# One schedule of attention groups over all blocks, with more of the transposes moved from TensorE to the DMA

## The chip, the cores and the metric

The kernel runs on one NeuronCore of a Trainium2 chip. The metric is device time in microseconds (us), the median of several executions. The engines that matter are TensorE (PE, whose weight loads are listed as PEld), VectorE (DVE), ScalarE (ACT) and SyncE (SP), which here only issues DMAs. Each engine works through its own instructions in the order of the program.

## What is computed

The reference chains three stages on 2304 tokens of width 512.

```python
# 1. attention in chunks of 64 tokens, 4 batches x 8 heads x 576 tokens x 64
scores = scale * q_c @ k_c^T ; scores -= max ; attn = exp(scores)
attn = attn / (sum(attn) + 1e-9) ; out = attn @ v_c
# 2. MLP1, d_ff = 2048
h = x @ w_in ; g = max(h, 0) + alpha * min(h, 0) ; x = g @ w_out
# 3. MLP2, d_ff = 1536
x = ((x @ w_a) * (x @ w_b)) @ w_out2
```

## The kernel before

**Precision by splitting.** Every matrix product of the MLPs is made of three matmuls, high times high, high times low and low times high (`three`, L366). A helper splits a float tile into a high part on ScalarE (`to_hi`, L79) and a low part on VectorE (`to_lo`, L82). The weights come as 64-bit numbers and are unpacked before they are split: ScalarE widens them (L124), VectorE does three steps (L128, L133, L136). A loaded weight tile of 512 KB is called a unit; there are 32 units for MLP1 and three staging buffers (tag `stg`) for units on their way.

**Blocks and steps.** The tokens are cut into five blocks of 512, 256, 512, 512 and 512 tokens. MLP1 runs block by block; a block has 16 steps `j`. In a step TensorE multiplies `x` with one column tile of `w_in` (`s1`, result in a PSUM bank `psh`), ScalarE and VectorE form the PReLU and its two parts (L384, L385, L386, then `gh` and `gl`), and TensorE multiplies these with a row tile of `w_out` two steps later (`s2`, into the four banks `acc`). During block 0 the step is `prelu_unpacking`: it also unpacks two units of weights, in an order written out by hand across ScalarE and VectorE, and loads two further ones. MLP2 follows for all blocks; the change does not touch it.

**Attention in groups.** 128 tokens are a group; there are 18 groups, numbered `u`, four in a block of 512 and two in block 1. For a group the kernel needs q and k transposed (`kT`, `qT`), scores (`att_S`, 32 small matmuls, L291), maximum and subtraction on VectorE (`att_M`), exponential on ScalarE (`att_X`, L312), normalization on VectorE (`att_N`, L317 to L321), the transpose of the result (`eT`, `att_PT`), and the product with v (`att_O`, 32 small matmuls, L342). The result is split into the `x` of its block.

**Two ways to transpose.** On TensorE, four transposes of 128x128 go to a PSUM bank and ScalarE copies that out (`att_T`, L278 and L280, for q and k; `att_PT`, L330 and L332, for e). Through the DMA, ScalarE first parts the 32-bit numbers into 16-bit halves (`halves`, L242, 128x1024), SP writes these to DRAM (L244), and a DMA transpose reads them back (`turned`, L249). Before the change groups 0 to 5 have q and k transposed on TensorE and groups 6 to 17 through the DMA (`apart`, then `turn_qk`); e is transposed on TensorE for groups 0 to 9 and through the DMA from `P_DMA = 10` on.

**Where the attention work stands.** The groups of block 0 come first, in an order written out by hand. The groups of block `b + 1` are worked on during the 16 steps of block `b`, at numbered slots, two in a step: an even slot `2j` is taken inside step `j`, in block 0 just behind the two PReLU reads of ScalarE, and an odd slot `2j + 1` at the end of the step, behind `s2`. `att_steps` gives the list of slots of one block; some actions return work that is done a little later in the step (`settle`). Block 0 takes the groups 4 and 5 (scores of both together in `both_S`, products of both in `both_O`), block 1 takes the groups 6 to 9 with a lag of one group between scores and product, and blocks 2 and 3 take four groups each with a lag of two.

**Buffers.** Four PSUM banks (`bank`) are shared by `psh`, the transposes and the pairs of banks of scores and products.

Of the kernel before, what the change touches and what calls it, by code (L numbers as in the profile page):

```python
# [8 lines left out]
F32 = mybir.dt.float32  # L9
# [9 lines left out]
def chunk_attention_prelu_mlp_bilinear_mlp(  # L19
# [18 lines left out]
    P = 128  # L38
# [29 lines left out]
    def bank(nm="ps"):  # L68
        return ps_p.tile([P, DM], F32, tag="ps", name=nm)
# [5 lines left out]
    def wtile(name, dt=F32R):  # L75
        return wp.tile([P, DM], dt, tag="w", name=name)
# [88 lines left out]
    def weave(*chains):  # L165


        live, later = [], [iter(c) for c in chains]
        while live or later:
            if later:  # L170
                live.append(later.pop(0))
            live = [c for c in live if next(c, None) is not None]
# [26 lines left out]
    def half(i):  # L199
        return slice(i * CH, (i + 1) * CH)  # L200
# [29 lines left out]
    def load_v(u):  # L230
        load("v", u)
# [2 lines left out]

    P_DMA = 10

    def halves(src, dst, nm):

        d = dst.bitcast(U16).rearrange("p (t f) -> p t f", t=2)
        nc.scalar.activation(out=d, in_=src.bitcast(U16).rearrange("p (f t) -> p t f", t=2), func=AF.Copy)  # L242
        rows = dr.tile([P, 2, DM], U16, name=f"rows{nm}")
        nc.sync.dma_start(out=rows, in_=d)  # L244
        return rows

    def turned(rows, nm):
        t = wtile(nm, F32)
        nc.sync.dma_start_transpose(  # L249
            out=t.bitcast(U16).rearrange("p (g r) -> p g r", g=KD), in_=rows.rearrange("p t f -> (p t) f")  # L250
        )
        return t
# [5 lines left out]
    def turn_qk(u):  # L258
        for nm, rows in zip("kq", att.pop(("rows", u))):
            t = turned(rows, f"{nm}T{u}")  # L260
            att[nm + "T", u] = lambda r, g, c, t=t: t[r, half(2 * g + c)]

    n_early = [0]

# [46 lines left out]
    def att_X(u):  # L311
        nc.scalar.activation(out=att["e", u], in_=att["e", u], func=AF.Exp, scale=SCALE)  # L312
# [9 lines left out]

    def att_PT(u):
        e_ = att.pop(("e", u))
        if u >= P_DMA:
            att["eT", u] = turned(halves(e_, wtile(f"ed{u}", F32), f"e{u}"), f"eT{u}")
            return
        ps = att_bank(u, "psP")
        for g in range(KD):
            nc.tensor.transpose(ps[:, g * P:(g + 1) * P], e_[:, g * P:(g + 1) * P], ident)  # L330
        t = wtile(f"eT{u}", F32)
        nc.scalar.activation(out=t, in_=ps, func=AF.Copy)  # L332
        att["eT", u] = t
# [18 lines left out]
    def each(fn, parts):  # L352
        for part in parts:
            fn(*part)
# [150 lines left out]
        while len(pend) > lag:  # L505
            pend.pop(0)()

    def att_steps(b, x):

        t0, n = blocks[b]
        us = range(t0 // P, (t0 + n) // P)

        def multiply(w, lag):
            pss = [bank("psSO") for _ in range(2)]
            now, before = us[w:w + 1], us[max(w - lag, 0):max(w - lag + 1, 0)]
            for u in now:
                att_S(u, [ps[:, :KD * CH] for ps in pss])
            o = []  # L520
            for u in before:
                o += att_O(u, *x, u * P - t0, [ps[:, KD * CH:] for ps in pss])
                if u + 2 < NU:
                    load_v(u + 2)
            each(to_hi, o)

            def then():
                for u in now:
                    att_M(u)
                each(to_lo, o)  # L530

            return then

        def soften(u):
            att_X(u)
            return lambda: weave(att_N(u))

        def both(product, us):
            pss = [bank("psSO") for _ in range(2)]
            return [product(u, [ps[:, i * KD * CH:(i + 1) * KD * CH] for ps in pss]) for i, u in enumerate(us)]  # L540

        def both_S():
            both(att_S, us)
            return lambda: att_M(us[0])

        def both_O(us):
            o = sum(both(lambda u, pss: att_O(u, *x, u * P - t0, pss), us), [])
            each(to_hi, o)
            for u in us:
                if u + 2 < NU:  # L550
                    load_v(u + 2)
            return lambda: each(to_lo, o)

        def nothing():
            pass

        def only(fn, *a):
            def step():
                if a[0] < NU:
                    fn(*a)  # L560
                return nothing

            return step

        if b == 1:
            u0, u1 = us
            return [
                (8, only(att_T, u0)),
                (10, only(att_T, u1)),
                (10, only(load_kq, u1 + 1, False)),  # L570
                (14, both_S),
                (16, lambda: lambda: att_M(u1)),
                (18, lambda: soften(u0)),
                (20, lambda: soften(u1)),
                (21, only(apart, u1 + 1, False)),
                (24, only(att_PT, u0)),
                (24, only(att_PT, u1)),
                (24, only(turn_qk, u1 + 1)),
                (25, only(load_kq, u1 + 2)),
                (27, lambda: both_O(us)),  # L580
                (28, only(apart, u1 + 2)),
                (29, only(load_kq, u1 + 3)),
                (30, only(turn_qk, u1 + 2)),
            ]
        u = us[0]
        if sizes[b - 1] < NB:
            S_, lag = {
                "m": (0, 7, 14, 21, 28), "s": (2, 9, 16, 23), "p": (6, 13, 20, 27),
                "l": ((4, 3), (11, 4), (18, 5), (29, 6)), "a": ((1, 2), (8, 3), (15, 4), (24, 5)), "t": ((4, 2), (11, 3), (25, 4), (29, 5)),
            }, 1  # L590
        else:
            S_, lag = {
                "m": (0, 6, 12, 18), "s": (2, 8, 14, 20), "p": (4, 10, 16, 22),
                "l": ((3, 3), (9, 4), (15, 5), (24, 6)), "a": ((1, 2), (7, 3), (15, 4), (23, 5)), "t": ((3, 2), (13, 3), (21, 4), (29, 5)),
            }, 2
        steps = [(slot, lambda w=w: multiply(w, lag)) for w, slot in enumerate(S_["m"])]
        steps += [(slot, lambda w=w: soften(us[w])) for w, slot in enumerate(S_["s"])]
        steps += [(slot, only(att_PT, us[w])) for w, slot in enumerate(S_["p"])]
        if lag == 2:
            steps += [(28, lambda: both_O(us[-2:]))]  # L600
        for i, fn in enumerate((load_kq, apart, turn_qk)):
            steps += [(slot, only(fn, u + n)) for slot, n in S_["lat"[i]]]
        return sorted(steps, key=lambda s: s[0])

    with tc.manual_schedule():
# [57 lines left out]
        to_hi(*wparts[3])  # L663
        nc.scalar.mul(nalpha_sb, alpha_sb, -1.0)

        for b, (t0, n) in enumerate(blocks):
            nxt = xtiles("x")
            steps = att_steps(b + 1, nxt) if b + 1 < NBLK else []

            def advance(slot, steps=steps):  # L670
                rest = []
                while steps and steps[0][0] <= slot:
                    rest.append(steps.pop(0)[1]())
                return rest

            def settle(rest):
                for then in rest:
                    then()

            for j in range(J1):  # L680
                if b == 0:
                    if j in (1, 3):
                        load_qk(n0 + j // 2)
                    if j in (4, 6):
                        load_v(n0 + j // 2 - 2)
                h = h0[0][:, :n] if not (b or j) else s1(j, x, n)
                if b == 0:
                    g = prelu_unpacking(j, h, lambda: w_dma(min(2 * j + 9, NU1)), lambda: advance(2 * j), settle)
                else:
                    rest = advance(2 * j)  # L690
                    g = prelu(j, h)
                    settle(rest)

                def second(b=b, j=j, g=g, n=n, nxt=nxt):
                    if j == 0:
                        acc[0] = new_acc()
                    s2(j, g, acc[0], n)
                    if j == J1 - 1:
                        end1(b, acc[0], n, nxt)

                pend.append(second)
                flush(2)
                settle(advance(2 * j + 1))
                if b == NBLK - 1 and j >= 2:
                    ready = NU1 + 3 * (j - 2) // 2
                    w_dma(ready + 3)
                    w_unpack(ready + 1)
                    w_split(ready)
            x = nxt
# [60 lines left out]
```

## Time and profile before

| | |
|---|---|
| median of 3 runs | 897.88 us (897.57 to 898.58) |
| the profiled execution | 897.61 us, span 895.8 us |
| TensorE | 884.1 us busy, 99% |
| VectorE, ScalarE | 402.7 us and 352.6 us, 45% and 39% |
| DMA | 79.48 MB, mean 89 GB/s |

The page divides the span into 40 slices of 22.4 us; attention and the unpacking of MLP1's weights lie in the first 16 or so, and behind them TensorE works alone. Block 0 of MLP1 runs from about 25 us to 118 us, block 1 to 173 us. A granted TensorE clock of 1.00 is the full 2.4 GHz.

### The profile page before, as it was taken

The numbers are of one execution on the slowest core, as the hardware profiler recorded it, in microseconds if no ns is written. First come the engines' busy times: TensorE is split into PE (matmuls) and PEld (weight loads), VectorE is DVE, ScalarE is ACT, GpSimd is POOL, SyncE is SP. The second block draws the span as 40 slices with busy tenths as digits, with TensorE's granted clock in tenths as the row PEclk, the third lists the DMA queues.
The fourth block names the chain that finished last, engine by engine and source line by source line (L and its number), as shares of the span: only waits on it lengthen the run. The fifth ranks groups of instructions, "written<-read, shape, count | busy, mean of one in ns | idle before, by whom it ended". The sixth has DMA issues, their size and how long they took to land.

```text
span 895.8 us, 12893 instructions
## 1 busy us (share of the span) xinstructions
PE 884.1 (99%) x5298; PEld 743.9 (83%) x5298; DVE 402.7 (45%) x762; ACT 352.6 (39%) x636; POOL 0.7 (0%) x6
## 2 busy tenths in 40 slices
PE   7999999999999999999999999999999999999998
PEld 6878889988888888888888888888888888888897
DVE  5999955454434443388756742111211122111221
ACT  5687765555436343466534422111211122111211
POOL 0000000000000000000000000000000000000000
PEclk9899999999999999999999999999999999999999
DMA  9686767455425320444414312000020002000100
GB/s 213 199 263 196 213 165 178 107 155 129 106 60 146 79 56 5 141 142 141 148 64 136 124 46 93 2 1 0 1 95 1 0 1 71 1 1 0 48 1 23
DMA packets 127498, 79.48 MB, mean 89 GB/s; under 512 B 94160, under 2 KB 116176, under 8 KB 127440
## 3 DMA queue, kind: packets, MB, share of 16 engines
q1 hardware_dynamic: 127152, 78.41, 31.0%
q8 instruction: 41, 0.67, 0.3%
q10 hardware_dynamic: 288, 0.26, 0.1%
q14 instruction: 17, 0.14, 0.1%
HBM read 53.49 MB, written 16.78 MB: 78 GB/s over the span
## 4 chain that ended last, share of the span: by engine, by line
PE 92%; DVE 6%; ACT 2%; issue 1%; ACTq 0%; POOLq 0%; DVEq 0%; POOL 0%
PE psh L366 52%; PE acc L366 37%; DVE wx L136 1%; PE psSO L291 1%; PE psSO L342 1%; DVE wz L128 1%; DVE wz L133 1%; DVE gl L82 0%; PE psT L278 0%; DVE sm L317 0%; PE warm L625 0%; PE psP L330 0%; DVE e L321 0%; DVE mx L304 0%; DVE e L306 0%
## 5 line engine op out<-in xcount | busy, mean ns | idle before, releaser
L442 DVE TENSOR_TENSOR b_sb<-psh,b_sb 128x512 f32<-128x512 f32 (+1 forms) x60 | 38.3, 638 | 273.2 <-PE psh L366 273.2
L386 DVE SCALAR_TENSOR_TENSOR pos<-neg,nalpha_sb,pos 128x512 f32<-128x512 f32 (+1 forms) x80 | 55.6, 695 | 107.3 <-ACT pos L385 107.0
L440 ACT ACTIVATE b_sb<-psh 128x512 f32<-128x512 f32 (+1 forms) x60 | 33.1, 552 | 168.2 <-PE psh L366 168.2
L79 ACT ACTIVATE ch<-b_sb 128x512 fp32r<-128x512 f32 (+1 forms) x60 | 35.3, 589 | 153.6 <-DVE b_sb L442 153.6
L82 DVE TENSOR_TENSOR gl<-pos,gh 128x512 fp32r<-128x512 f32 (+1 forms) x80 | 51.1, 638 | 43.5 <-ACT gh L79 43.5
L79 ACT ACTIVATE gh<-pos 128x512 fp32r<-128x512 f32 (+1 forms) x80 | 47.2, 590 | 59.0 <-DVE pos L386 59.0
L384 ACT ACTIVATE neg<-psh 128x512 f32<-128x512 f32 (+1 forms) x80 | 43.8, 548 | 40.4 <-PE psh L366 40.4
L82 DVE TENSOR_TENSOR cl<-b_sb,ch 128x512 fp32r<-128x512 f32 (+1 forms) x60 | 38.3, 639 | 39.3 <-ACT ch L79 39.3
L136 DVE SCALAR_TENSOR_TENSOR wx<-wx,wz 128x512 int32<-128x512 int32 x68 | 46.8, 689 | 4.7 <-ACT wx L124 0.8
L124 ACT ACTIVATE wx<-raw 128x512 f32<-128x512 f32 x68 | 42.7, 669 | 4.0 <-DMA raw<-in_moe_w_b_dram 3.8
L385 ACT ACTIVATE pos<-psh 128x512 f32<-128x512 f32 (+1 forms) x80 | 44.2, 553 | 0.0
L128 DVE TENSOR_SCALAR wz<-raw 128x512 uint16<-128x512 uint16 x68 | 29.8, 462 | 3.2 <-DMA raw<-in_moe_w_b_dram 3.2
L133 DVE TENSOR_SCALAR wz<-raw 128x512 uint16<-128x512 uint16 x68 | 31.0, 455 | 0.0
L242 ACT ACTIVATE kqd<-kq 128x1024 uint16<-128x1024 uint16 x24 | 23.9, 1047 | 0.3 <-DMA kq<-in_k_dram 0.3
L79 ACT ACTIVATE xh<-psSO 128x256 fp32r<-128x256 f32 x28 | 8.9, 384 | 25.0 <-PE psSO L342 25.0
L312 ACT ACTIVATE e<-e 128x512 f32<-128x512 f32 x18 | 11.3, 629 | 13.6 <-DVE e L306 13.4
L242 ACT ACTIVATE ed<-e 128x1024 uint16<-128x1024 uint16 x8 | 8.5, 1058 | 17.2 <-DVE e L321 13.6
L321 DVE TENSOR_TENSOR e<-e,rc 128x512 f32<-128x512 f32 x18 | 12.4, 691 | 0.6
L317 DVE TENSOR_REDUCE sm<-e 128x8 f32<-128x512 f32 x18 | 12.2, 680 | 1.0 <-ACT e L312 0.8
L82 DVE TENSOR_TENSOR xl<-psSO,xh 128x256 fp32r<-128x256 f32 x28 | 10.2, 415 | 1.5 <-ACT xh L79 1.5
L304 DVE TENSOR_REDUCE mx<-psSO 128x4 f32<-128x256 f32 x28 | 10.5, 418 | 0.7 <-ACT xh L79 0.7
L291 PEld LDWEIGHTS psSO<-kT,qT 64*64 64x64 f32 x448 | 7.7, 134 | 3.7 <-issue 2.8
(731 smaller groups left out, 2505.7 us busy)
## 6 DMA issues: line engine op xcount, KB each, us to landing
raw<-in_moe_w_out_dram SPq DMA_DIRECT2D x28, 512.0 KB, 3.5
raw<-in_moe_w_in_dram SPq DMA_DIRECT2D x16, 512.0 KB, 4.6
raw<-in_moe_w_b_dram SPq DMA_DIRECT2D x12, 512.0 KB, 4.7
raw<-in_moe_w_a_dram SPq DMA_DIRECT2D x12, 512.0 KB, 3.8
v<-in_v_dram SPq DMA_DIRECT2D x16, 256.0 KB, 4.2
out_dram<-os SPq DMA_DIRECT2D x8, 512.0 KB, 2.8
rowsk<-kqd SPq DMA_DIRECT2D x12, 256.0 KB, 2.1
rowsq<-kqd SPq DMA_DIRECT2D x12, 256.0 KB, 2.5
```

What stands on the lines that cost most here:

```text
L79: nc.scalar.activation(out=hi, in_=src, func=AF.Copy)
L82: nc.vector.tensor_tensor(out=lo, in0=src, in1=hi.bitcast(F32), op=ALU.subtract)
L124: return nc.scalar.activation(out=x.bitcast(F32), in_=hw.bitcast(F32), func=AF.Copy, scale=2.0 ** -112)
L128: yield nc.vector.tensor_scalar(out=z2[:, :, 0], in0=h2[:, :, 1], scalar1=13, scalar2=None, op0=ALU.logical_shift_right)
L133: yield nc.vector.tensor_scalar(out=z2[:, :, 1], in0=h2[:, :, 3], scalar1=1 << 15, scalar2=None, op0=ALU.bitwise_and)
L136: yield nc.vector.scalar_tensor_tensor(out=x, in0=x, scalar=3, in1=z, op0=ALU.logical_shift_left, op1=ALU.bitwise_or)
L366: nc.tensor.matmul(out=ps, lhsT=a, rhs=b, start=(i == 0 and first), stop=(i == n_i - 1 and a is wl))
L384: nc.scalar.activation(out=neg, in_=h, func=AF.Relu, scale=-1.0)
L385: yield nc.scalar.activation(out=pos, in_=h, func=AF.Relu)
L386: yield nc.vector.scalar_tensor_tensor(out=pos, in0=neg, scalar=nalpha_sb[:, j:j + 1], in1=pos, op0=ALU.mult, op1=ALU.add)
L440: nc.scalar.activation(out=b_sb, in_=pb, func=AF.Copy)
L442: nc.vector.tensor_tensor(out=b_sb, in0=pa, in1=b_sb, op=ALU.mult)
```

## The change

The two functions of a list of slots per block become one function, `att_schedule`, with one line of slots over all blocks (32 slots to a block, `PER`). In it:

- q and k of groups 4 and 5 are loaded with `load_kq` where `load_qk` was, and transposed through the DMA: `apart` at slots 6 and 9, `turn_qk` at slots 8 and 11. `att_T` is left to block 0.
- e goes through the DMA from group 6 on (`apart_e`, `turn_e` as steps of their own); `att_PT` is left to groups 0 to 5.
- The scores of groups 4 and 5 move from slot 14 to 16, `att_M` of 5 from 16 to 17. `apart` of 6 moves from slot 21 to 18, of 7 from 28 to 25, and that of group 8 into block 0 (slot 30). The first scores of block 1's work (group 6) move from slot 32 to 31.
- From group 6 on every scores step carries the product of the group two before, across the borders of blocks; the last scores of a block's work no longer stand at its beginning, and `both_O` at the end of blocks 2 and 3 is gone.
- In a joint step the low parts of the product come before `att_M`, where they came behind it.

```diff
-    P_DMA = 10
+    def apart_e(u):
+        att["rows_e", u] = halves(att.pop(("e", u)), wtile(f"ed{u}", F32), f"e{u}")
+
+    def turn_e(u):
+        att["eT", u] = turned(att.pop(("rows_e", u)), f"eT{u}")
...
     def att_PT(u):
         e_ = att.pop(("e", u))
-        if u >= P_DMA:
-            att["eT", u] = turned(halves(e_, wtile(f"ed{u}", F32), f"e{u}"), f"eT{u}")
-            return
...
+    PER = 2 * J1
+    def multiply(now, before):
+        pss = [bank("psSO") for _ in range(2)]
+        if now is not None:
+            att_S(now, [ps[:, :KD * CH] for ps in pss])
+        o = []
+        if before is not None:
+            o = outputs(before, [ps[:, KD * CH:] for ps in pss])
+        each(to_hi, o)
+
+        def then():
+            each(to_lo, o)
+            if now is not None:
+                att_M(now)
+        return then
...
+        u = sizes[0] // P
+        do(6, apart, u, False)
+        do(8, turn_qk, u)
+        do(9, apart, u + 1, False)
+        do(11, turn_qk, u + 1)
+        do(10, load_kq, u + 2, False)
+        at(16, both_S, u, u + 1)
+        at(17, lambda: lambda: att_M(u + 1))
+        do(18, apart, u + 2, False)
+        at(18, soften, u)
+        do(21, turn_qk, u + 2)
+        at(20, soften, u + 1)
+        do(20, load_kq, u + 3, False)
+        do(24, att_PT, u)
+        do(24, att_PT, u + 1)
+        do(25, apart, u + 3)
+        do(26, turn_qk, u + 3)
+        at(27, both_O, u, u + 1)
+        do(28, load_kq, u + 4)
+        do(30, apart, u + 4)
+        at(31, multiply, u + 2, None)
+        at(36, multiply, u + 3, None)
...
+        when = {u + 3: 31}
+        for b in range(1, NBLK - 1):
+            us = [w for w in range(NU) if group_block[w] == b + 1]
+            for w, s in zip(us, (11, 17, 23, 29) if sizes[b] < NB else (8, 15, 22, 29)):
+                when[w + 2] = b * PER + s
+        for w, s in list(when.items())[1:]:
+            at(s, multiply, w if w < NU else None, w - 2)
+            if w >= NU:
+                continue
+            at(s + 2, soften, w)
+            do(s + 4, apart_e, w)
+            if w > u + 4:
+                do(when[w - 1] + 1, turn_qk, w)
+            do(s + 8, turn_e, w)
+            if w > u + 5:
+                do(when[w - 2] + 3, apart, w)
+            if w > u + 6:
+                do(when[w - 3] + 4, load_kq, w)
...
                     if j in (1, 3):
-                        load_qk(n0 + j // 2)
+                        load_kq(n0 + j // 2, False)
```

## Rows read from the trace of the kernel before

**Rows 1.** The page, part 1: busy us (share of the span) and instructions.
```profile
PE 884.1 (99%) x5298; PEld 743.9 (83%) x5298; DVE 402.7 (45%) x762; ACT 352.6 (39%) x636; POOL 0.7 (0%) x6
```

**Rows 2.** Busy time by stretch: length, PE, PEld, DVE, ACT, POOL, clock, DMA share, GB/s.
```profile
45.00:70.00 25.00, 24.37 (x174) 19.87 (x173) 24.06 (x47) 19.69 (x36) 0.00 (x0) 1.00 0.90 265
70.00:95.00 25.00, 25.00 (x112) 20.72 (x111) 24.77 (x53) 17.24 (x32) 0.00 (x0) 1.00 0.53 172
...
135.00:173.00 38.00, 38.00 (x452) 37.40 (x452) 21.40 (x54) 22.62 (x53) 0.00 (x0) 1.00 0.71 160
```

**Rows 3.** Timeline of PE in block 0: start, us, work, wait before it.
```profile
47.76 0.60 PE L278 MATMUL psT<-ident,k 128*128 128x128 f32 x4
...
48.55 0.48 PE L366 MATMUL acc<-gh,wo2h 128*128 128x512 f32 x1
...
54.89 0.66 PE L278 MATMUL psT<-ident,k 128*128 128x128 f32 x4 [0.63 <-ACT pos L385]
...
55.79 0.48 PE L366 MATMUL acc<-gh,wo3h 128*128 128x512 f32 x1
...
96.29 0.63 PE L330 MATMUL psP<-ident,e 128*128 128x128 f32 x4 [0.40 <-DVE e L321]
```

**Rows 4.** Chain of waits, pieces in order of time: start, us, what.
```profile
93.77 0.60 DVE wx L136
94.38 0.61 DVE sm L317
...
95.45 0.70 DVE e L321
96.15 0.14 issue
96.29 0.63 PE psP L330 x4
```

**Rows 5.** Timeline of DVE and ACT in block 0.
```profile
49.96 0.74 DVE L386 SCALAR_TENSOR_TENSOR pos<-neg,nalpha_sb,pos 128x512 f32<-128x512 f32 x1
...
54.72 0.60 ACT L280 ACTIVATE kT<-psT 128x512 f32<-128x512 f32 x1
...
55.19 0.74 DVE L386 SCALAR_TENSOR_TENSOR pos<-neg,nalpha_sb,pos 128x512 f32<-128x512 f32 x1
...
55.68 1.26 ACT L124 ACTIVATE wx<-raw 128x512 f32<-128x512 f32 x2
...
59.84 0.59 ACT L385 ACTIVATE pos<-psh 128x512 f32<-128x512 f32 x1
...
60.79 0.73 DVE L386 SCALAR_TENSOR_TENSOR pos<-neg,nalpha_sb,pos 128x512 f32<-128x512 f32 x1
...
66.38 0.74 DVE L386 SCALAR_TENSOR_TENSOR pos<-neg,nalpha_sb,pos 128x512 f32<-128x512 f32 x1
```

**Rows 6.** Timeline of ACT: two halves, and two widenings at two places.
```profile
65.90 1.46 ACT L124 ACTIVATE wx<-raw 128x512 f32<-128x512 f32 x2
...
71.14 1.24 ACT L124 ACTIVATE wx<-raw 128x512 f32<-128x512 f32 x2
...
94.95 1.99 ACT L242 ACTIVATE kqd<-kq 128x1024 uint16<-128x1024 uint16 x2
```

**Rows 7.** Timeline near the end of block 0, DVE and PE.
```profile
117.49 0.69 DVE L82 TENSOR_TENSOR gl<-pos,gh 128x512 fp32r<-128x512 f32 x1 [0.70 <-ACT gh L79]
...
119.28 0.50 PE L366 MATMUL acc<-gh,wo14h 128*128 128x512 f32 x1
```

**Rows 8.** DMA issues: what, count, KB each, median us to landing.
```profile
rowsk<-kqd SPq DMA_DIRECT2D x12, 256.0 KB, 2.1
...
kT<-rowsk SPq DMA_TRANSPOSE x12, 4.0
qT<-rowsq SPq DMA_TRANSPOSE x12, 3.5
```

**Rows 9.** Chain of waits around block 1, pieces in order of time.
```profile
118.73 0.62 PE psSO L291 x32
...
142.79 0.44 PE psP L330 x4
...
145.28 0.47 PE psSO L342 x32
145.75 1.63 PE acc L366 x12
147.38 1.44 PE psh L366 x12
```

**Rows 10.** Timeline of DVE and PE at the start of block 2.
```profile
186.31 0.75 DVE L459 COPY xs<-acc 128x256 f32<-128x256 f32 x2
...
186.78 0.50 PE L366 MATMUL acc<-gh,wo0h 128*128 128x512 f32 x1
```

More of the change, by code (lines that the diff above doesn't have):

```diff
@@ L506, in flush @@
             pend.pop(0)()
[L508 to L602, printed above, removed]
@@ new lines, in chunk_attention_prelu_mlp_bilinear_mlp @@
+    PER = 2 * J1
+    group_block = [b for b, n in enumerate(sizes) for _ in range(n // P)]
+    xof = {}
+    def multiply(now, before):
[11 more added lines that the diff above has]
+        return then
@@ new lines, in outputs, with soften, both_S, both_O @@
+    def outputs(u, pss):
+        b = group_block[u]
+        o = att_O(u, *xof[b], u * P - blocks[b][0], pss)
+        if u + 2 < NU:
+            load_v(u + 2)
+        return o
+    def soften(u):
+        att_X(u)
+        return lambda: weave(att_N(u))
+    def both_S(*us):
+        pss = [bank("psSO") for _ in range(2)]
+        for i, u in enumerate(us):
+            att_S(u, [ps[:, i * KD * CH:(i + 1) * KD * CH] for ps in pss])
+        return lambda: att_M(us[0])
+    def both_O(*us):
+        pss = [bank("psSO") for _ in range(2)]
+        o = []
+        for i, u in enumerate(us):
+            o += outputs(u, [ps[:, i * KD * CH:(i + 1) * KD * CH] for ps in pss])
+        each(to_hi, o)
+        return lambda: each(to_lo, o)
@@ new lines, in att_schedule, with at, do @@
+    def att_schedule():
+        steps = []
+        def at(slot, fn, *a):
+            steps.append((slot, lambda: fn(*a)))
+        def do(slot, fn, *a):
+            steps.append((slot, lambda: fn(*a) and None or (lambda: None)))
+        u = sizes[0] // P
[20 more added lines that the diff above has]
+        at(36, multiply, u + 3, None)
+        do(37, turn_qk, u + 4)
+        at(33, soften, u + 2)
+        do(33, load_kq, u + 5)
+        at(38, soften, u + 3)
+        do(35, apart_e, u + 2)
+        do(40, apart_e, u + 3)
+        do(37, turn_e, u + 2)
+        do(39, apart, u + 5)
+        do(42, turn_e, u + 3)
+        do(40, load_kq, u + 6)
+        when = {u + 3: 31}
[16 more added lines that the diff above has]
+                do(when[w - 3] + 4, load_kq, w)
@@ L664, in chunk_attention_prelu_mlp_bilinear_mlp, with advance @@
         nc.scalar.mul(nalpha_sb, alpha_sb, -1.0)
+        steps = att_schedule()
         for b, (t0, n) in enumerate(blocks):
-            nxt = xtiles("x")
-            steps = att_steps(b + 1, nxt) if b + 1 < NBLK else []
-            def advance(slot, steps=steps):
+            nxt = xof[b + 1] = xtiles("x")
+            def advance(slot, t=b * PER):
                 rest = []
-                while steps and steps[0][0] <= slot:
+                while steps and steps[0][0] <= t + slot:
                     rest.append(steps.pop(0)[1]())
```

## The prediction

> **What bounds the kernel now.** I began with the page's busy shares: TensorE is busy for 99% of the span and the other engines for less than half [rows 1]. Read alone, this says that whatever is taken off TensorE is gained. That holds only where TensorE does not wait for someone else soon after, so the second view is the busy time by stretches [rows 2]. From 45 to 95 us, in block 0, VectorE is busy for 24.06 and 24.77 of each 25 us: there it is as full as TensorE. From 135 to 173 us, in block 1, TensorE has 38.00 of 38.00 us and VectorE only 21.40. So there are two regimes, and the change works in both.
>
> The third view is the chain of waits. In block 0 it runs through VectorE (unpacking, normalization) up to e of group 5, which ends at 96.15 us, and there TensorE takes it over with the transposes of e, for which it had waited [rows 3, 4]. So at 96 us, behind the whole stretch of unpacking, TensorE's place in time is set by VectorE. What TensorE saves earlier in block 0 turns into a longer wait at this point; what delays VectorE earlier moves the point back.
>
> In block 1 the chain is TensorE's own work, piece behind piece [rows 9].
>
> **The change, part by part.**
>
> *Transposes of q and k of groups 4 and 5 off TensorE.* They take 48.55 - 47.76 = 0.79 us for the one group and 0.63 + 0.90 us for the other, the 0.63 being a wait for a bank; with 0.1 us of slower start of the matmuls behind each the sum is 2.5 us [rows 3]. I count this as 0, because TensorE meets e of group 5 afterwards. The cover is VectorE's fullness; if that is gone, it is worth -2.5.
>
> *What ScalarE gets instead.* A pair of evictions of transposes goes and a pair of halves comes, for each group. In the hand-written order of block 0 both engines form one loop: VectorE's `pos` of one step to that of the next. A step without evictions takes 55.19 - 49.96 = 5.23 us; the two with evictions take 5.60 and 5.59 us [rows 5]. So the evictions cost the loop 0.73 us in all, which is now saved. A pair of halves takes 1.99 us [rows 6].
> - Group 4, slot 6: the halves stand where the evictions stood, before the two widenings. The evictions held ScalarE there for 55.68 - 54.72 = 0.96 us and the loop grew by 0.36, so 0.60 us was free [rows 5]. The halves cost 1.99 - 0.60 = 1.39.
> - Group 5, slot 9: the halves stand before ScalarE's PReLU reads. In the step there ScalarE's `pos` ended at 59.84 + 0.59 = 60.43 and VectorE took it at 60.79, so 0.36 us was free [rows 5]; cost 1.99 - 0.36 = 1.63.
>
> Together 1.39 + 1.63 - 0.73 = +2.3 us on e of group 5. Scores and maximum of these groups come two slots later, but the same VectorE work still lies before the normalization at slots 18 and 20, so no further shift. `apart` of 6 at slot 18 falls into a step in which VectorE has both maxima to do; I count it 0, as before at slot 21, where it lay beside the normalization. Nothing hides 2.3: VectorE has 0.23 us idle in the 25 us to 95 us [rows 2]. Bounds: -0.7 (ScalarE's idle 5.3 of 25 us takes all halves) and +2 x 1.99 = 4.0.
>
> *The DMAs beside them.* Four writes of rows and four DMA transposes of 256 KB each, 2.10 MB, are issued between about 50 and 70 us. The DMA engines are busy there for 0.90 at 265 GB/s, which makes 294 GB/s when full [rows 2]: the new transfers take 7.1 us, and 2.5 us of the 25 are free. A loop that runs 2.3 us later gives 2.3 more. 2.3 us remain by which loads of weights come late. These loads have no room: at 65.90 two widenings took 1.46 us where the same pair takes 1.24 at 71.14, so ScalarE already waited there for a unit [rows 6]. SP is passed in order as well: the transposes wait for the landing of the rows (2.1 us) and take 3.5 to 4.0 to land themselves [rows 8], with the next load queued behind. Half of the units are used a step later than the other half, so I take 1.5 of the 2.3. Bounds: 0, and 7.1 - 2.5 = 4.6.
>
> The Trainium skill, in VectorE: DVE Perf Modes, section Rules for kernel authors, advises TensorE for a 128x128 transpose when PSUM will do as the destination, and its section The three transpose paths puts the crossbar DMA at 1309 ns against 390 ns. By these figures the 32 16-bit blocks of the four new transposes of q and k would take an estimated 32 x 1.309 = 42 us one after the other; no such wait fits the rows, where one DMA transpose of eight such blocks lands 3.5 to 4.0 us after its issue [rows 8].
>
> *Halves of group 7 at slot 25.* They now fall before the last step that unpacks: again 1.63 on the loop. The `gl` that this delays ended at 117.49 + 0.69 = 118.18 and TensorE used it at 119.28, so 1.1 us is free [rows 7]: +0.5. Bounds 0 and 1.6.
>
> *Transposes of e of groups 6 to 9 off TensorE.* Four times 0.44 us in block 1 [rows 9], where TensorE never stops: -1.8. The halves and DMAs that come instead stand beside ScalarE's 15.4 idle us of 38 and a DMA share of 0.71 [rows 2]; the results are needed eight slots or more after the halves. I take the whole gain. Bounds: -1.8, and +4 if the DMAs run out (a rival below).
>
> *One line of groups.* Scores alone cost 0.62 us, a product in the same step 0.47 more, and the first run of matmuls behind such a step 1.63 where 1.44 is usual [rows 9]. Behind groups 4 and 5 there were 15 such steps (six single, seven joint, two of two products, which I cost like a joint one), now 14 (four single, ten joint): 13.5 us against 13.4, and one slower start of 0.2 less: -0.3.
>
> *Start of block 2.* TensorE waited there for the copies of `acc`, which stood behind the normalization of group 10 on VectorE [rows 10]; that now comes earlier. -0.3, between -0.6 and 0.
>
> Everything else (order of low parts and maximum, steps in blocks 2 and 3, loads that only change place) I cost at 0: already in block 1 ScalarE and VectorE are idle for 40% and 44% [rows 2], and in blocks 2 and 3 a slot has twice the tokens and so about twice the time. If that cover is gone, a step that comes late costs what rival 3 gives it.
>
> **Sum.** +2.3 + 1.5 + 0.5 - 1.8 - 0.3 - 0.3 = +1.9 us. The profiled execution took 897.61 us, the median is 897.88; I add to the median: 899.8 us. The end of the kernel is TensorE alone, so a shift of TensorE at the end of block 0 reaches the end unchanged.
>
> **The rivals.**
>
> *Rival 1, TensorE's savings all count (the other side).* If VectorE's loop does not decide at 96 us, 2.5 + 1.8 + 0.3 + 0.3 = 4.9 us are gained: 893.0 us. For it: 99% busy. Against it: TensorE's wait for e [rows 3] and VectorE's 24.77 of 25 us. It decides from the point where e of group 5 is ready 2.5 us before TensorE comes to it; now it is late. Chance 0.10.
>
> The Trainium skill, in Perfetto Trace Analysis, section Identifying the Most-Contended Engine, says to improve the engine with the highest occupancy first, TensorE judged by its weight loads; with PEld at 83% [rows 1] that is TensorE and gives rival 1's time. The stretches show where the rule stops: from 70 to 95 us VectorE is at 99% and PEld at 83% [rows 2].
>
> *Rival 2, ScalarE's gaps swallow the halves.* Then e comes 0.7 us earlier, the loads are in time and block 1 gains as worked out: -0.7 - 1.8 - 0.3 - 0.3 = -3.1, 894.8 us. For it: ScalarE is idle for 5.3 of 25 us [rows 2]. Against it: an eviction pair of 0.96 us already cost 0.36. Chance 0.20, about 0.06 of it ending within 0.2% of before.
>
> *Rival 3, the DMAs of block 1 run out.* In six slots of 1.44 us (plus scores and product, 10 us in all) a group now moves nine transfers of 256 KB: 2.36 MB, 8.0 us at 294 GB/s, beside the writes of block 0's result. If scores wait 1 us for `kT` four times, that is +4 on top: 903.8 us. Against it: eT and kT have several slots of room. Chance 0.14, 0.02 of it within 0.2%.
>
> **How the numbers follow.** A run of this kernel can tell about 0.2%, 1.8 us, from no change. My forecast has 0.56; with its bounds for the loads alone it spans 898.3 to 902.9 us, and 0.22 of its chance lies below 899.7, that is within 0.2%. Faster: 0.10 + 0.14 = 0.24. Same: 0.22 + 0.06 + 0.02 = 0.30. Slower: 0.34 + 0.12 = 0.46. The range leaves out rival 1 and the upper part of rival 3: 894.4 to 903.4.
>
> **What would show it.** In the changed trace: 32 transposes of q and k and 24 of e on TensorE, none of e in block 1. VectorE's e of group 5 near 98.5 us or up to 2 later instead of 96.15, and TensorE idle for several us before the transposes of group 5 (2.5 it has saved, and 2.3 or more of lateness). ScalarE or VectorE waiting for `raw` between 60 and 80 us. Two steps of VectorE's loop of 6.6 and 6.9 us where halves stand. TensorE still full in block 1. The prediction is wrong if e of group 5 ends before 96 us, or if TensorE waits in block 1 for `kT` or `eT`.

## The result, and the profile after

The changed kernel takes 904.37 us (903.66 to 904.79), the kernel before beside it 897.73 us: ratio 1.0075, 95% interval 1.0063 to 1.0087. It is slower by 6.6 us: the sign was forecast, but the time lies 1 us above the forecast range (up to 903.4). The profiled execution took 904.79 us, its span is 903.0 us.

The page of the changed kernel, busy shares ([rows 1] has them before) and the chain of work that ended last:

```profile
PE 883.7 (98%) x5266; PEld 741.9 (82%) x5266; DVE 403.9 (45%) x762; ACT 355.5 (39%) x636; POOL 0.7 (0%) x6
...
PE 85%; DVE 7%; ACT 3%; DMA 3%; issue 1%; ACTq 0%; POOLq 0%; DVEq 0%; POOL 0%
PE psh L367 49%; PE acc L367 33%; DMA raw<-in_moe_w_out_dram 3%; DVE wx L136 2%; DVE gl L82 1%; DVE wz L133 1%; PE psSO L343 1%; ACT kqd L240 1%; DVE wz L128 1%; PE psSO L295 1%; DVE e L310 0%; DVE mx L308 0%; DVE xl L82 0%; ACT neg L385 0%; ACT pos L386 0%
```

The same chain line before the change:

```profile
PE 92%; DVE 6%; ACT 2%; issue 1%; ACTq 0%; POOLq 0%; DVEq 0%; POOL 0%
```

The busy shares say almost nothing. The chain says more: before, no DMA stands in it; now 3% of the span, over 20 us, runs through the landing of `raw`, the weights on their way. The stretches of block 0 and block 1 say where (columns as in [rows 2], with which they compare):

```profile
45.00:70.00 25.00, 21.83 (x91) 16.93 (x90) 19.86 (x38) 18.27 (x31) 0.00 (x0) 0.98 1.00 251
70.00:95.00 25.00, 23.61 (x157) 18.99 (x156) 21.68 (x46) 17.37 (x30) 0.00 (x0) 0.96 0.85 243
142.00:180.00 38.00, 37.47 (x525) 36.45 (x524) 23.45 (x59) 27.41 (x60) 0.00 (x0) 1.00 0.95 229
```

From 45 to 70 us the DMA engines are full (1.00, before 0.90), and yet they move 251 GB/s where they moved 265. VectorE, full before, is idle for 5 of 25 us. What it and ScalarE wait for stands in the waits of 45 to 105 us (total us, times, longest):

```profile
ACT wx L124 <- DMA raw<-in_moe_w_out_dram: 7.7, 5, 2.3
DVE wz L128 <- DMA raw<-in_moe_w_out_dram: 5.2, 3, 2.1
...
PE psP L331 <- DVE e L325: 3.3, 1, 3.3
```

ScalarE's timeline shows one such place, behind the halves of group 5 (start, us, work, wait before it):

```profile
60.65 1.99 ACT L240 ACTIVATE kqd<-kq 128x1024 uint16<-128x1024 uint16 x2
62.54 0.58 ACT L385 ACTIVATE neg<-psh 128x512 f32<-128x512 f32 x1
63.02 0.59 ACT L386 ACTIVATE pos<-psh 128x512 f32<-128x512 f32 x1
63.49 0.67 ACT L124 ACTIVATE wx<-raw 128x512 f32<-128x512 f32 x1
66.51 0.68 ACT L124 ACTIVATE wx<-raw 128x512 f32<-128x512 f32 x1 [2.35 <-DMA raw<-in_moe_w_out_dram]
```

SP's timeline shows why this load came late: it was issued at 61.38, behind two DMA transposes, the first of which held SP for 4.67 us.

```profile
55.27 4.67 SPq L247 DMA_TRANSPOSE kT<-rowsk  x1
60.05 1.23 SPq L247 DMA_TRANSPOSE qT<-rowsq  x1
61.38 0.53 SPq L100 DMA_DIRECT2D raw<-in_moe_w_out_dram  x1
```

In the kernel before, the load of this step went out 1.21 us behind VectorE's `pos` (56.40 against 55.19), here 4.62 us (61.38 against 56.76). A plain load can be held as well: one of `raw`, at 65.63, kept SP for 3.89 us.

The loop of VectorE passes this lateness on until e of group 5, which ends at 104.28 us instead of 96.14, and TensorE, early by now, waits for it (timeline of DVE and PE, to compare with the last row of [rows 3] and with e in [rows 4]):

```profile
103.59 0.69 DVE L325 TENSOR_TENSOR e<-e,rc 128x512 f32<-128x512 f32 x1
...
104.43 0.63 PE L331 MATMUL psP<-ident,e 128*128 128x128 f32 x4 [3.28 <-DVE e L325]
```

### The profile page after: what moved, and what is told of

The parts are those of the page before. It is cut to its first block, busy times and chain, and to the rows that moved or that the text cites. A ratio compares the mean times of both kernels' runs of the same rounds, so it can differ in the third digit from the quotient of the medians.

```text
span 903.0 us, 12820 instructions
## 1 busy us (share of the span) xinstructions
PE 883.7 (98%) x5266; PEld 741.9 (82%) x5266; DVE 403.9 (45%) x762; ACT 355.5 (39%) x636; POOL 0.7 (0%) x6
## 3 DMA queue, kind: packets, MB, share of 16 engines
q1 hardware_dynamic: 136752, 82.60, 33.3%
## 4 chain that ended last, share of the span: by engine, by line
PE 85%; DVE 7%; ACT 3%; DMA 3%; issue 1%; ACTq 0%; POOLq 0%; DVEq 0%; POOL 0%
PE psh L367 49%; PE acc L367 33%; DMA raw<-in_moe_w_out_dram 3%; DVE wx L136 2%; DVE gl L82 1%; DVE wz L133 1%; PE psSO L343 1%; ACT kqd L240 1%; DVE wz L128 1%; PE psSO L295 1%; DVE e L310 0%; DVE mx L308 0%; DVE xl L82 0%; ACT neg L385 0%; ACT pos L386 0%
## 5 line engine op out<-in xcount | busy, mean ns | idle before, releaser
L240 ACT ACTIVATE kqd<-kq 128x1024 uint16<-128x1024 uint16 x28 | 27.9, 1045 | 0.0
L240 ACT ACTIVATE ed<-e 128x1024 uint16<-128x1024 uint16 x12 | 12.6, 1048 | 4.4 <-DVE e L325 3.7
L295 PE MATMUL psSO<-kT,qT 64*64 64x64 f32 x448 | 9.7, 224 | 1.6 <-DMA qT<-rowsq 1.4
```

## The experiments

Two theories stood against each other. **A**: the DMAs of groups 4 and 5 make weight loads late, and these hold the loop of VectorE and ScalarE. **B**: ScalarE's halves hold it. Beside them **C**, a form of A in which it is SP's order and not the DMA engines; and **D**, that block 1 runs out of DMA time (rival 3).

All timings, in us. "e5" is the end of e of group 5 in the profiled execution (before: 96.14). The next columns are TensorE's place against the profiled kernel before: "at e", lateness at the transposes of e of group 5 (96.29 before); "behind e", what is added up to the first matmul of step 15 of block 0 (111.69); "block 1", what that block and the start of block 2 add, up to step 4 of block 2 (194.57); "sum", all three. From that point to the end TensorE's shift changes by less than 0.1. The 1.5 or 1.6 "behind e" of five runs go with a lower granted clock, told of in the last section. The profiled execution is one of those timed and lies up to 1.6 us from the median of its kernel.

| run | median | ratio to before, 95% interval | e5 | at e | behind e | block 1 | sum |
|---|---|---|---|---|---|---|---|
| changed kernel | 904.37 | 1.0075 (1.0063 to 1.0087) | 104.28 | 8.1 | 0.0 | -1.0 | 7.1 |
| 1 groups 4, 5 on TensorE | 897.76 | 1.0003 (0.9994 to 1.0011) | 96.59 | 0.4 | 0.0 | -0.2 | 0.3 |
| 2 their DMA path alone | 906.17 | 1.0101 (1.0084 to 1.0117) | 103.62 | 7.5 | 0.0 | 0.0 | 7.5 |
| 3 halves alone | 900.74 | 1.0037 (1.0025 to 1.0049) | 100.26 | 4.1 | 1.6 | -2.2 | 3.5 |
| 4 DMAs alone | 904.66 | 1.0077 (1.0065 to 1.0089) | 102.52 | 6.4 | 1.6 | -1.1 | 6.9 |
| 5 loads first | 904.73 | 1.0077 (1.0064 to 1.0089) | 103.12 | 7.0 | 1.5 | -1.4 | 7.1 |
| 6 plain reads | 899.10 | 1.0020 (1.0011 to 1.0029) | 97.53 | 1.4 | 0.0 | -0.3 | 1.1 |
| 7 one line alone | 898.94 | 1.0016 (1.0007 to 1.0025) | 96.69 | 0.5 | 0.0 | 1.1 | 1.7 |
| 8 earlier turns | 899.81 | 1.0029 (1.0019 to 1.0039) | 96.53 | 0.4 | 0.0 | 1.7 | 2.1 |
| 9 other loads moved | 900.17 | 1.0028 (1.0018 to 1.0039) | 98.62 | 2.5 | 1.6 | -1.5 | 2.6 |
| 10 one line, later | 897.56 | 1.0000 (0.9991 to 1.0009) | 96.17 | 0.0 | 0.0 | -0.2 | -0.2 |
| 11 e of 8, 9 on TensorE | 897.08 | 0.9994 (0.9986 to 1.0003) | 96.38 | 0.2 | 0.0 | 0.3 | 0.6 |
| 12 group 4 alone by DMA | 900.52 | 1.0037 (1.0024 to 1.0049) | 100.19 | 4.0 | 1.6 | -1.0 | 4.6 |
| 13 loads on GpSimd | 903.53 | 1.0070 (1.0048 to 1.0093) | 101.26 | 5.1 | 0.0 | 0.7 | 5.8 |
| 14 control to 13 | 898.29 | 1.0006 (0.9998 to 1.0015) | 97.56 | 1.4 | 0.0 | 0.3 | 1.8 |
| 15 kept busy | 901.34 | 1.0039 (1.0027 to 1.0051) | 98.70 | 2.6 | 0.0 | 1.9 | 4.5 |

Runs 5, 9, 12 and 13 are the changed kernel with the edit shown; run 1 too, and runs 3, 4, 6, 7, 8, 10, 11 and 14 are run 1 with a further edit; run 15 is run 9 with one; run 2 starts from the kernel before. The cuts of code show the lines that matter; `...` stands for others.

**1. Which part of the change costs.**

```diff
-        do(6, apart, u, False)
-        do(8, turn_qk, u)
-        do(9, apart, u + 1, False)
-        do(11, turn_qk, u + 1)
+        do(8, att_T, u)
+        do(10, att_T, u + 1)
...
-                        load_kq(n0 + j // 2, False)
+                        load_qk(n0 + j // 2)
```

> The changed kernel with q and k of groups 4 and 5 transposed on TensorE again (evictions at slots 8 and 10); the one line of groups and e of groups 6 to 9 through the DMA stay. Theory A (the eight new DMAs of groups 4 and 5 fill the DMA engines between 50 and 80 us, weight loads come late and hold the unpacking loop): e of group 5 ends near 96.2 us as in the kernel before, and the rest of the change keeps its gain, 0.5 - 1.8 - 0.3 - 0.3 = -1.9: 895.8 us. Theory B (ScalarE's halves hold the loop): the same here. Rival D (the DMAs of block 1 cost what they save, the loss sits in e of groups 6 to 9): e of group 5 is early, but the total stays at 898 us or above.

e of group 5 is back, the whole loss is gone, but the gain of 1.9 us that A expected is not there. Groups 4 and 5 cost the 6.6 us; the rest of the change is worth nothing in this run.

**2. The same part by itself**, in the kernel before.

```diff
-                (8, only(att_T, u0)),
-                (10, only(att_T, u1)),
+                (6, only(apart, u0, False)),
+                (8, only(turn_qk, u0)),
+                (9, only(apart, u1, False)),
+                (11, only(turn_qk, u1)),
...
-                (14, both_S),
-                (16, lambda: lambda: att_M(u1)),
+                (16, both_S),
+                (17, lambda: lambda: att_M(u1)),
...
```

> The kernel before with this part of the change alone: q and k of groups 4 and 5 through the DMA at the slots of the change, their scores at 16. Theories A and B: e of group 5 ends near 104 us, as in the changed kernel, and the whole +8 reaches the end, since the gain in block 1 is missing: 905 to 906 us. Rival D (the loss sits in block 1): within 1 us of the kernel before.

906.17 us, 0.2 above what A and B expected, and e of group 5 ends at 103.62. Groups 4 and 5 on the DMA are the loss with or without the one line.

**3 and 4. Halves without DMAs, DMAs without halves.**

```diff
+        do(6, halves_alone, u)
         do(8, att_T, u)
+        do(9, halves_alone, u + 1)
         do(10, att_T, u + 1)
...
```

> As the first kernel of this call (groups 4 and 5 on TensorE), with ScalarE's four halves of groups 4 and 5 added at slots 6 and 9 and their results not used: no row writes, no DMA transposes. The evictions stay as well. Theory B (the halves are the cost): e of group 5 moves by most of the 8.1 us, to 102 to 104. The recorded sum: 1.39 + 1.63 = +3.0, e of group 5 near 99.2 us, and the total 3 us above the first kernel. Theory A with halves that fit into ScalarE's gaps: 0 to +1.

```diff
+        do(6, rows_alone, u)
+        do(8, turn_alone, u)
         do(8, att_T, u)
+        do(9, rows_alone, u + 1)
         do(10, att_T, u + 1)
+        do(11, turn_alone, u + 1)
...
```

> As the first kernel of this call (groups 4 and 5 on TensorE), with the four row writes and the four DMA transposes of groups 4 and 5 added at the slots of the change, without ScalarE's halves (the rows are written as they are loaded) and with their results not used. Theory A (the DMA engines and the loads behind them are the cost): e of group 5 moves by 5 to 8 us, to 101 to 104, and the total with it. Theory B: by 0 to 1.5 us, which is the term of the recorded sum.

The halves move e of group 5 by 100.26 - 96.59 = 3.7 us, near the 3.0 of the recorded working, and the DMAs by 5.9, four times the recorded 1.5. Together they give 7.7 (104.28 - 96.59) and not 9.6. Both runs keep the evictions that the changed kernel saves, 0.7 us by the recorded working; that some of the halves' time lies under the waits for loads would give the rest, but no run shows it by itself.

**5. Another order on SP.**

```diff
-        do(8, turn_qk, u)
+        do(9, turn_qk, u)
...
-        do(10, load_kq, u + 2, False)
+        do(11, load_kq, u + 2, False)
```

> The changed kernel with the same DMAs in another order on SP: the DMA transposes of group 4 at slot 9 and the loads of q and k of group 6 at slot 11, so that both stand behind the two weight loads of their step instead of ahead of them. Bytes, halves and transposes are the same. Theory C (SP's queue in order: weight loads stand behind a DMA transpose whose issue alone took 4.67 us): only the halves' cost is left, e of group 5 ends near 100.3 us as with the halves alone, total 900 to 901 us. Theory A in its strict form (the DMA engines have no time left, whatever the order): e of group 5 stays at 103 to 104.5 us, total 903.5 to 904.5 us.

e of group 5 gains 1.2 us and the total nothing, since the lower clock behind e takes 1.5. This looked like the strict form of A, but the order was only half mended: the loads of step 6 still stood behind the transposes of group 5 (the second held SP from 67.33 to 70.82, and the first of these loads went out at 73.14). Runs 6 and 13 say more.

**6. The same bytes, not transposed.**

```diff
-            turned(att.pop(("rows", nm, u)), f"{nm}T{u}")
+            t = wtile(f"{nm}T{u}", F32)
+            nc.sync.dma_start(
+                out=t.bitcast(U16).rearrange("p (t f) -> p t f", t=2), in_=att.pop(("rows", nm, u))
+            )
```

The edit is shown as against run 4.

> As the kernel with the DMAs of groups 4 and 5 alone, with its four DMA transposes replaced by four plain reads of the same 256 KB rows into the same unused tiles: the same bytes, issued at the same places, nothing transposed. If the bytes are the cost: e of group 5 stays near 102.5 us and the total near 904.7 us. If the transposing itself is (its issue on SP, its many small packets): e of group 5 ends at 98 to 99.5 us and the total comes to 899.5 to 901 us.

e of group 5 ends at 97.53 us: the bytes cost 0.9 of the 5.9 us, the transposing 5.0, SP's longer issue included (the first pair held SP for 3.71 and 1.24 us in run 4, for 0.56 and 0.38 in run 6). From 55 to 65 us the DMA engines are full in both runs (the view's share can come out above 1; that is read as full) and move 230 GB/s in run 4 (first line), 348 in run 6 (second):

```profile
55.00:65.00 10.00, 10.00 (x49) 8.32 (x49) 6.58 (x14) 6.67 (x13) 0.00 (x0) 1.00 1.01 230
```

```profile
55.00:65.00 10.00, 10.00 (x49) 8.28 (x48) 8.64 (x18) 7.88 (x16) 0.00 (x0) 1.00 1.08 348
```

The page's line of SP's queue (packets, MB, share of 16 engines' span) gives the price under load, for runs 1, 4 and 6:

```profile
q1 hardware_dynamic: 131952, 80.50, 32.5%
```

```profile
q1 hardware_dynamic: 136752, 82.60, 33.6%
```

```profile
q1 hardware_dynamic: 133104, 82.60, 33.1%
```

Times the spans of 896.1, 902.7 and 896.9 us these are 291.2, 303.3 and 296.9 us of all engines: four writes and four plain reads take 5.7, four writes and four transposes 12.1. The shares are rounded, and each of the three times can be off by 0.45 us. A transpose of 256 KB thus takes 1.6 us more than a plain read of 256 KB, give or take 0.2, and 912 packets more ((136752 - 133104) / 4). Whether the packets, the transposing itself or SP's longer issue makes the loads late is not separated here. The Trainium skill says in Advanced Engine Details and Errata, section X-Bar Transpose (TRN2), that transposing DMAs are as fast as regular ones; these runs say otherwise.

**7 and 10. The one line without e on the DMA**, first with `att_PT` of groups 6 and 7 at slots 36 and 41, then at 38 and 42.

```diff
-        do(35, apart_e, u + 2)
-        do(40, apart_e, u + 3)
-        do(37, turn_e, u + 2)
+        do(38, att_PT, u + 2)
+        do(42, att_PT, u + 3)
...
-            do(s + 4, apart_e, w)
+            do(s + 4 if w > u + 5 else s + 7, apart_e if w > u + 5 else att_PT, w)
...
```

> The one line of groups alone: as the kernel with groups 4 and 5 on TensorE (897.76 us), and e of groups 6 to 9 on TensorE as well. By the recorded sum e through the DMA is worth -1.8, so this one would take 899.5 us. Rival D (in block 1 the waits for kT and eT eat what TensorE saves): within 0.5 us of 897.8, and TensorE's 1.5 us or so of waits in block 1 are gone.

> The one line of groups alone, as before with e of groups 6 to 9 on TensorE, but with the transposes of e of group 6 two slots later and of 7 one slot later, since TensorE waited 1.2 us for e of group 6 in the first form. Without that wait the first form's 898.94 us come to 897.5 to 897.9 us. Then e through the DMA in groups 6 to 9 is worth nothing against it (the kernel with it took 897.76); if it is worth the -1.8 of the recorded sum, this one stays at 899 us or above.

The first form waited 1.2 us for e of group 6, the second did not, and took 897.56 us, level with the kernel before and with run 1. So the one line is worth nothing, and against it e of groups 6 to 9 through the DMA nothing either, instead of -1.8.

**8 and 11. Block 1's waits.** Run 8 issues most of block 1's transposes earlier and moves the scores of group 7, with what follows them, two slots later; run 11 takes e of 8 and 9 off the DMA.

```diff
-                do(when[w - 1] + 1, turn_qk, w)
+                do(when[w - 2] + 5 if w > u + 5 else 42, turn_qk, w)
-            do(s + 8, turn_e, w)
+            do(s + 7, turn_e, w)
...
```

> As the kernel with groups 4 and 5 on TensorE, with the DMA transposes of block 1 issued earlier (q and k of groups 9 to 17 up to three slots, e from group 8 on one slot) and the scores of group 7 two slots later, away from the copies of block 0's result. Rival D in its weak form (block 1 loses about 2 us because transposes are issued late behind others on SP): 1 to 2 us less than 897.76, 895.8 to 896.8 us. If the DMA engines themselves are short of time in block 1: no better than 897.5 us.

> As the kernel with groups 4 and 5 on TensorE (897.76 us), with e of groups 8 and 9 on TensorE and of 6 and 7 still through the DMA. TensorE waited there 1.7 us in two places for the eT, kT or qT of groups 8 to 11; if the two DMA transposes of e caused that by their place on SP and their time on the DMA engines, 1.7 is saved and 2 x 0.45 spent: 897.0 us. If the waits come from kT and qT alone: 897.8 to 898.7 us.

Run 11's edit is the `att_PT` line of run 10, without its first half. Run 8 is worse: it has one wait of 2.5 us, for the `eT` of group 8. That transpose stands behind `kT` and `qT` of group 10 in both runs; in run 8 it was issued at 158.49, in run 1 at 157.84, and took 5.3 us to land where the longest in run 1 took 4.2. Run 11 has the lowest median, and its interval includes 1: no version here is shown to beat the kernel before. The waits of TensorE from 128 to 195 us, in run 8 and in run 3, whose block 1 runs by the same schedule as that of the changed kernel:

```profile
PE psSO L343 <- DMA eT<-rowse: 2.5, 1, 2.5
PE acc L367 <- ACT xs L461: 0.9, 1, 0.9
```

```profile
PE psSO L350 <- DMA eT<-rowse: 0.3, 1, 0.3
```

Where the waits are 0.3 us (run 3), block 1 gives -2.2; with 2.5 for `eT` it gives +1.7. TensorE's busy time over the stretch of the column "block 1" shows gain and loss apart, for the kernel before, run 1, the changed kernel and run 3 (first columns: length, PE busy):

```profile
111.69:194.57 82.88, 82.75 (x841) 75.71 (x840) 45.49 (x104) 50.22 (x106) 0.00 (x0) 1.00 0.61 147
```

```profile
112.17:194.86 82.69, 81.25 (x826) 74.26 (x824) 49.35 (x113) 52.49 (x109) 0.00 (x0) 1.00 0.84 201
```

```profile
119.85:201.71 81.86, 80.96 (x825) 74.18 (x824) 49.30 (x113) 52.34 (x109) 0.00 (x0) 1.00 0.82 204
```

```profile
117.42:198.09 80.67, 80.34 (x826) 74.06 (x824) 47.86 (x110) 52.00 (x107) 0.00 (x0) 1.00 0.87 204
```

Busy time falls by 1.5, 1.8 and 2.4 us: the gain is there. Idle time grows from 0.1 to 1.4, 0.9 and 0.3, which pays much of it back. In run 1, 0.8 of the 1.4 are waits for `eT` and `qT`; the others are for `xs`, the copies of block 0's result (0.3), and waits without a releaser (0.3).

**9. Room for the DMAs.**

```diff
-                    if j in (4, 6):
-                        load_v(n0 + j // 2 - 2)
+                    if j in (9, 11):
+                        load_v(n0 + j // 2 - 4)
...
-        do(10, load_kq, u + 2, False)
+        do(15, load_kq, u + 2, False)
```

> The changed kernel with 1.05 MB of other loads taken out of the crowded stretch: v of groups 4 and 5 in steps 9 and 11 where they stood in 4 and 6, q and k of group 6 at slot 15 where they stood at 10. If the time of the DMA engines between 50 and 80 us is the cost, 1.05 MB at the 294 GB/s of plain loads give back up to 3.6 us: e of group 5 ends near 101 us (not below 100.3, where the halves alone put it), total 900.8 to 902 us. If the chain of rows, DMA transposes and SP's order is the cost whatever else is loaded: e of group 5 stays at 103.5 to 104.5 us and the total at 904 us.

e of group 5 comes back to 98.62 us, farther than expected: the one wait for `raw` that is left has 0.7 us. So about +2.5 is what the halves cost when the evictions are gone and the loads are nearly in time, and the other 5.7 us of the changed kernel are the loads. The four DMA transposes are all still there: what costs 5.7 us is that they stand in a stretch that has no room for them beside the other loads. Whether the room is missing on the engines or on SP this run can't tell, since the moved loads left SP's queue as well.

**12. Half the step.**

```diff
-        do(9, apart, u + 1, False)
-        do(11, turn_qk, u + 1)
+        do(10, att_T, u + 1)
...
```

> The changed kernel with half of the disputed step: q and k of group 4 through the DMA, of group 5 on TensorE again. If the DMA engines' free time of 2.5 us has to be used up before anything is late, the two writes and two DMA transposes (4.65 us of all engines by the queue's shares) make e of group 5 late by about 2.2 us, and the halves' 1.8 lies beneath that: e of group 5 near 98.8 us, total 899.5 to 900.5 us. If each DMA transpose costs its share from the first on: half of 7.7, e of group 5 near 100.4 us, total 901 to 901.5 us.

e of group 5 at 100.19 speaks for a cost from the first transfer on; the median of 900.52 lies just above the range of the other theory. The profiled execution was the longest of its five. Left open.

**13 and 14. The loads on another queue.** Run 14 is run 1 with the same edit.

```diff
+        eng = nc.gpsimd if 8 <= i < NU1 else nc.sync
...
-            nc.sync.dma_start(out=raw, in_={"o": w_out, "p": w_o}[m][j * P:(j + 1) * P, :])
+            eng.dma_start(out=raw, in_={"o": w_out, "p": w_o}[m][j * P:(j + 1) * P, :])
...
```

> The changed kernel with the weight loads of MLP1 from the ninth unit on issued by GpSimd, so that no load stands behind a DMA transpose, a row write or another load in SP's order. If SP's order is what makes the loads late (each DMA transpose holds SP for 1.2 to 4.7 us): the waits for raw shrink to a third, e of group 5 ends near 99 us, total 899 to 901 us, less what the other queue itself costs in the control. If the time of the DMA engines is: e of group 5 stays at 102.5 to 104.5 us, 3 us or less from the changed kernel against the control.

> Control to the kernel before it: the same loads on GpSimd's queue, with groups 4 and 5 on TensorE. If the other queue is as good as SP's: 897.8 us and e of group 5 near 96.6 us, as with SP. What lies above that is the queue's own cost.

Between the theories: against the control e of group 5 is late by 3.7 us, not 7.7. With the halves' 2.5 us of run 9 taken off, an estimated 1.2 us of that are loads, where the changed kernel has 5.7: SP's order is a large part. But loads that stood behind no transpose in GpSimd's queue still landed late: ScalarE waited 5.8 us for `raw`, in the control 2.7, in the changed kernel 7.7. TensorE waited 3.7 us for `qT` of the scores, and the medians differ by 5.2 us, with scatter. That both causes act fits this; their shares are not settled.

**15. The clock behind the wait.**

```diff
+        do(24, keep_busy, 24)
         do(24, att_PT, u + 1)
...
```

> As the changed kernel with the loads moved out of the stretch (900.17 us, where TensorE waited 3.1 us for e of group 5 and then ran about 4 us at a granted clock of 0.50), with 24 transposes of the identity into an unused bank put between the transposes of e of group 4 and 5, 2.6 us of TensorE time inside that wait; nothing reads them. If the lower clock after the wait is what puts 1.6 us on top of the lateness of e: the clock stays at 1.00 and the total comes to 898.6 us. If not: 900 us or more.

The clock stayed at 1.00 and the 1.6 us behind e are gone. The total missed the expected 898.6 us and is 1.2 above run 9's: TensorE then waited 2.3 us in block 1 for a `qT`, and that column went from -1.5 to +1.9. The cause of the loss behind e was right, the sum wrong; why block 1 lost so much here is not shown.

## Why the prediction was wrong

It forecast +1.9 us; the medians differ by 6.6 us, the profiled executions, from which the terms below are read, by 7.2.

- **Halves of groups 4 and 5 on ScalarE, +2.3**: right. Run 9 shows 2.5, with 0.7 us of wait for `raw` still in it. The first two steps of VectorE's loop with halves, forecast at 6.6 and 6.9 us, took 56.76 - 50.26 = 6.50 and 63.64 - 56.76 = 6.88.
- **The DMAs beside them, +1.5**: the step that failed, with the right mechanism and the wrong size. It measured 8.14 - 2.47 = 5.7 us (lateness at e of the changed kernel and of run 9), above its own bound of 4.6. The sum took 2.10 MB at 294 GB/s. A DMA transpose doesn't go at that rate, and the trace of before said so: alone on the engines, two transposes (first window below) take 8.00 x 0.40 = 3.20 us of all engines, two row writes of the same size (second) 4.50 x 0.32 = 1.44:

```profile
254.00:262.00 8.00, 8.00 (x95) 6.46 (x94) 2.78 (x6) 3.47 (x9) 0.00 (x0) 1.00 0.40 68
269.50:274.00 4.50, 4.50 (x22) 3.72 (x21) 1.89 (x5) 3.27 (x5) 0.00 (x0) 1.00 0.32 117
```

  Four of each are 9.3 us, not 7.1; under load 12.1 (run 6). Then 2.5 us of idle share and 2.3 us for a later loop were taken off, and the rest was cut to 1.5 of 2.3. With 12.1 in place of 7.1 the same deductions give an estimated (12.1 - 2.5 - 2.3) x 1.5 / 2.3 = 4.8, not far from 5.7: it was the price of the transposes that failed, more than the room taken off. SP's order, which the prediction names, had no term of its own; the first new transpose held SP for 4.67 us, and run 13 makes this a large part, so how much of the 5.7 is engine time stays open. Block 1's row in [rows 2] carried the same warning: 160 GB/s at 0.71 is 225 GB/s when full, where block 0 gave 294.
- **PE's saved transposes counted 0**: right. TensorE waits 3.28 us for e of group 5.
- **Halves of group 7, +0.5**: about right, as far as it shows; TensorE's lateness grows from 8.16 at step 15 of block 0 to 8.51 at step 2 of block 1, +0.35, in which the halves' part is not separated.
- **e of groups 6 to 9 off TensorE and one line, -1.8 - 0.3 - 0.3**: somewhat over half of it came, 7.14 - 8.51 = -1.4 in the changed kernel. TensorE's idle time in block 1 grew (run 8's section), in part by waits for `eT` (0.3 us here, 0.6 in run 1), which the forecast listed as a sign of its failure. Runs 1 and 10 differ by 0.2 us in the median: -1.8 was too much.
- Rivals 1 and 2 fell: no saving counted before 96 us, and ScalarE's gaps did not swallow the halves. Rival 3 was right in kind, but its +4 did not come: block 1 still gained.

In terms: +2.5 + 5.7 + 0.35 - 1.4 = +7.2, which is the profiled difference. That it closes proves nothing, since all terms but the split between 2.5 and 5.7 are steps of one shift; that split rests on run 9, and run 4's 5.9 for the DMAs alone agrees. That the sign was right is no credit to the sum: it was +1.9 from terms of which the largest loss was sized at about a quarter.

The Trainium skill's advice in VectorE: DVE Perf Modes, section Rules for kernel authors, to transpose 128x128 on TensorE where PSUM will do, was the better guide for groups 4 and 5. The 42 us that the prediction worked out from that page's figure, as a serial wait, did not appear; the four transposes with their writes took 12.1 us of the engines.

## What to carry to other kernels

Price a DMA by the time it holds the DMA engines and its issuing queue, read where it runs alone, not by its bytes at the rate of other transfers: a DMA transpose here holds the engines for more than twice the time of a plain transfer of its size. The price grows beside other traffic: four writes and four transposes come to 9.3 us alone and to 12.1 in the full stretch. Where an in-order queue carries the loads of a full engine, ask also what stands behind the new transfer in that queue. And follow a gain to the next place where the same queue is used: block 1 gave back part of what it saved, in run 1 nearly all.

## What the hardware showed that was not expected

Behind a wait of TensorE for e of group 5 the granted clock fell in five runs (3, 4, 5, 9 and 12). Run 9 waited 3.10 us, and its windows from 98 to 104 us show the clock at 0.50, the 1.2 GHz level, from 100 to 102:

```profile
98.00:100.00 2.00, 1.24 (x6) 1.17 (x7) 2.00 (x4) 1.62 (x4) 0.00 (x0) 0.77 1.42 179
100.00:102.00 2.00, 2.00 (x6) 1.52 (x6) 2.00 (x6) 0.63 (x1) 0.00 (x0) 0.50 1.06 216
102.00:104.00 2.00, 2.00 (x9) 1.64 (x8) 2.00 (x4) 0.95 (x2) 0.00 (x0) 0.87 1.01 228
```

Matmuls that start 0.23 us apart at 1.00 start 0.43 apart there, and 1.6 us are lost. Run 15 filled 2.78 us of the same wait with transposes, the clock stayed at 1.00 (second kernel, same stretch) and the loss was gone:

```profile
98.00:100.00 2.00, 1.36 (x9) 1.06 (x8) 1.99 (x4) 1.71 (x4) 0.00 (x0) 1.00 1.46 208
100.00:102.00 2.00, 2.00 (x10) 1.66 (x9) 2.00 (x6) 0.63 (x1) 0.00 (x0) 1.00 1.03 211
102.00:104.00 2.00, 2.00 (x11) 1.65 (x10) 2.00 (x4) 0.86 (x2) 0.00 (x0) 1.00 0.73 182
```

The changed kernel waited 3.28 us at the same place and kept 1.00; what decides is not settled here. Its clock fell earlier: from 70 to 72 us it was 0.50, behind a wait of TensorE of 2.60 us for `gh`, and that loss lies under the later wait for e.
